# Two more feed-forward steps before the inverse-transform stage, and a different spread of start-up work, in an FFT-mixing and feed-forward kernel

## Chip, cores and metric

One Trainium2 chip, one of its cores. The metric is the device time of one execution in microseconds, the median of several runs. The engines are named as in the profile: PE is TensorE's matmuls, PEld its weight loads, DVE VectorE, ACT ScalarE, POOL GpSimd, SP SyncE (here it only issues transfers).

## What is computed

Eight batches of 3072 tokens with 256 channels. Each batch goes through a real FFT over its tokens, a complex 256x256 channel mix with bias and soft threshold, an inverse FFT, and then a feed-forward block of width 2048:

```python
X = np.fft.rfft(x, axis=1)
Yr = Xr @ w_r - Xi @ w_i + b_r
Yi = Xr @ w_i + Xi @ w_r + b_i
Y  = soft_threshold(Yr, 0.01) + 1j * soft_threshold(Yi, 0.01)
y  = np.fft.irfft(Y, n=3072, axis=1)
h  = y @ w_in                      # 256 -> 2048
out = (h * np.tanh(softplus(h))) @ w_out   # 2048 -> 256
```

`w_in` and `w_out` are in double precision, the rest in float32.

## The kernel before

The FFT of one batch is written as four stages of small matmuls, held as lists of items by `chain(b)`, with the result of each of the first three stages stored to a scratch in DRAM and read back in another order:

- Stage one (items A, 7 of two matmul groups): loads x, writes the scratch `s1`. PSUM tile `psa`.
- Stage two (12 items B, each followed one item later by an item M that mixes the channels): reads `s1`, multiplies (`psb`, then `psk` and `psp`, or `psm` in the first batch), adds bias, thresholds on DVE (L481 to L483), and stores `y` to the scratch `s3`: four transfers for most items (L572).
- Stage three (13 items C): each reads `s3` with four transfers (L612), is split on DVE into a high part (`hi`, L195) and a low part (`lo`, L198), multiplied (`psc`, three matmuls, L634), copied by ACT and stored to `s2`.
- Stage four (12 items F, called columns here): one transfer from `s2` (L652) and one of constants `vt`; a split on DVE; matmuls `psf` (L677, L678); then on DVE `eo`, `yt` and `yl` (L681 to L687), with ACT's `cor` and `yh` in between. This gives the activations `yh`, `yl` of the feed-forward block.

All products of float32 values are built from a high and a low part, so splits on DVE precede most matmuls.

The feed-forward block of the current batch runs at the same time as the FFT of the next one. The main loop counts steps `t`, 96 for a batch (six chunks of tokens by 16 slices of the width 2048). A step issues, in this order: `ffn1` (six matmuls into `hp`, L759, then an activation `s` on ACT); every second step `split_g` (the split of `s` into `gh` and `gl` on DVE, L773 and L774, a pair of steps at a time); then one piece of the FFT; then `ffn2` of four steps earlier (twelve matmuls into `acc`, L790). The FFT pieces come from two generators made by `run_chain`. `extra` brings one column of the current batch's FFT; two are created in each of five chunks (`tt % 16` is 2 or 8). Its loads are issued at creation, its split three steps later, its matmuls two steps after that. `gen` brings stages one to three, and the first two columns, of the next batch. In a step in which `extra` issues its matmuls, `gen` is not advanced.

`run_chain` walks the stages. At the start of a stage it issues the first loads (three items ahead), then yields some empty steps, in which only feed-forward work is issued; then it issues the first two splits, yields again, and then issues one item's matmuls per step, with the loads three and the splits two items ahead. The number of empty steps is this line; `k == 2` is stage three, and `gap` is 2 in the main loop:

```python
for _ in range(gap + (2 if k == 2 else 1 if last else 0) if gap else 0):
    yield None
```

So four empty steps stand before the first splits of stage three, and one between them and its first matmuls. This place occurs seven times, in the FFTs of batches 2 to 8, during the feed-forward work of batches 1 to 7. The FFT of the first batch runs alone ahead of the main loop, with `gap=0`. DVE works on the feed-forward weights in that time: `aux_steps(n)` issues n small DVE operations that turn double-precision weights (`raw`) into high and low parts in `win` and `wout`, 97 of them at most. `on_seg(k)` issues a fixed number at a stage's start, and `PACE[k]` is the number per piece of stage k. `aux_load`, `load_mix` and `load_bias` issue the transfers of raw weights (POOL), mixing weights (SP) and bias (POOL).

Of the kernel before, what the change touches and what calls it, by code (L numbers as in the profile page):

```python
# [127 lines left out]
def fft_mix_ffn_kernel(ctx: ExitStack, tc: tile.TileContext, x, w_r, w_i, b_r, b_i, w_in, w_out,  # L128
# [35 lines left out]
    def f32(ap):  # L164
        return ap.bitcast(F32)
# [27 lines left out]
    def split(src, hi, lo, eng="v"):  # L193
        if eng == "v":
            nc.vector.tensor_copy(out=hi, in_=src)  # L195
        else:
            nc.scalar.activation(out=hi, in_=src, func=ACTF.Copy)  # L197
        nc.vector.tensor_tensor(out=lo, in0=src, in1=f32(hi), op=ALU.subtract)  # L198
# [10 lines left out]
    def setup_dft():  # L209
        nc.gpsimd.dma_start(out=fa, in_=c_fa)  # L210

    def setup_u():
        nc.gpsimd.dma_start(out=uu, in_=c_u)
# [3 lines left out]
    def load_mix():  # L217
        for k in range(2):
            t = p_y.tile([128, 2, 512], F32, tag=("yh", "yl")[k], name="wraw").rearrange("p a f -> p (a f)")[:, 0:512]
            nc.sync.dma_start(out=t[:, 0:256], in_=w_r[k * 128:(k + 1) * 128, :])  # L220
            nc.sync.dma_start(out=t[:, 256:512], in_=w_i[k * 128:(k + 1) * 128, :])
            mixraw.append(t.rearrange("p (s c) -> p s c", s=2))

    def load_bias():
        nc.gpsimd.dma_start(out=bias[:, 0, :], in_=b_r.rearrange("(o c) -> o c", o=1).to_broadcast([128, DM]))
        nc.gpsimd.dma_start(out=bias[:, 1, :], in_=b_i.rearrange("(o c) -> o c", o=1).to_broadcast([128, DM]))

    def setup_mix():
        for k in range(2):
            src = mixraw[k]  # L230
            hi, lo = wmix[:, k, 0, 1:3, :], wmix[:, k, 1, 1:3, :]
            split(src, hi, lo, "s")
            for s in range(2):
                nc.scalar.activation(out=wmix[:, k, s, 0, :], in_=f32(wmix[:, k, s, 2, :]), func=ACTF.Copy, scale=-1.0)
# [63 lines left out]
    def weight_jobs():  # L298
        def w1(k, n):
            sl = slice(n * 512, (n + 1) * 512)  # L300
            return (w_in.bitcast(I32)[k * 128:(k + 1) * 128, n * 1024:(n + 1) * 1024],
                    *(win[:, k, s, sl].rearrange("p (a c) -> p a c", a=2) for s in range(2)), False)

        def w2(n):
            return (w_out.bitcast(I32)[n * 256:(n + 1) * 256, :].rearrange("(k p) c -> p k c", p=128),
                    *(wout[:, 2 * n:2 * n + 2, s, :] for s in range(2)), True)

        order = [w1(0, 0), w1(1, 0), w1(0, 1), w1(1, 1), w2(0), w2(1), w1(0, 2), w1(1, 2), w2(2), w2(3),
                 w1(0, 3), w1(1, 3), w2(4), w2(5), w2(6), w2(7)]
        return [FromDouble(n, *a) for n, a in enumerate(order)]  # L310
# [15 lines left out]
    def tick():  # L326
        while pend:
            pend.pop(0)()
# [378 lines left out]
    def run_chain(segs, ahead_n=3, ahead_a=2, cla=2, gap=0, hold=None, on_seg=None):  # L707


        for k, seg in enumerate(segs):  # L710
            while hold is not None and k == len(segs) - 1 and hold():
                yield None
            n = len(seg)
            at = [0, 0, 0]
            la, pla = (ahead_a, 1) if k == 0 and n == 7 else (ahead_n, 2)

            def ahead(i):
                for s, (d, f) in enumerate(((la, "load"), (cla, "cload"), (pla, "prep"))):
                    while at[s] < min(n, i + d):
                        getattr(seg[at[s]], f)()  # L720
                        at[s] += 1

            while at[1] < min(n, cla):
                seg[at[1]].cload()
                at[1] += 1
            while at[0] < min(n, la):
                seg[at[0]].load()
                at[0] += 1
            if on_seg is not None:
                on_seg(k)  # L730
            last = k == len(segs) - 1
            for _ in range(gap + (2 if k == 2 else 1 if last else 0) if gap else 0):
                yield None
            while at[2] < min(n, pla):
                seg[at[2]].prep()
                at[2] += 1
            for _ in range((2 if last or k == 1 else 1) if gap else 0):
                yield None
            for i in range(n):
                ahead(i + 1)  # L740
                for f in seg[i].mm:
                    tick()
                    f()
                    yield k
            tick()
# [59 lines left out]
    with tc.manual_schedule():  # L805
        setup_dft()
        aux = weight_jobs()
        n_raw = [0]

        def aux_load(m):  # L810
            while n_raw[0] < min(m, len(aux)):
                aux[n_raw[0]].load()
                n_raw[0] += 1

        def aux_run():
            for n, job in enumerate(aux):
                aux_load(n + 1)
                for k, _ in enumerate(job.work(aux[n - 1] if n else None)):
                    if k == 5:
                        aux_load(min(n + (4 if n + 3 <= N_EARLY else 3), 16 if started[0] else N_EARLY + 1))  # L820
                    yield
            yield from aux[-1].finish()

        aux_gen = aux_run()
        n_aux = [0]

        def aux_steps(m):
            for _ in range(m):
                if started[0] or n_aux[0] < 9 * N_EARLY - 2:
                    next(aux_gen, None)  # L830
                    n_aux[0] += 1

        def on_seg(k):
            if k == 1:
                setup_mix()
                aux_steps(4)
            elif k == 2:
                aux_steps(12)
            elif k == 3:
                aux_steps(10)  # L840

        PACE = (1.6, 0.9, 1.6, 2)
        first = chain(0)
        cnt = 0
        owed = 0.0
        for k in run_chain(first, ahead_n=6, ahead_a=3, cla=3, on_seg=on_seg):
            cnt += 1
            if cnt in (2, 5, 9):
                aux_load(1 + (cnt > 2) + 2 * (cnt > 5))
            if cnt == 7:  # L850
                load_mix()
                load_bias()
            if cnt == 11:
                for it in first[1][:3]:
                    it.cload()
            if cnt == 20:
                setup_u()
            if cnt == 57:
                for it in first[3]:
                    it.cload()  # L860
            if cnt > 4:
                owed += PACE[k]
            while owed >= 1:
                aux_steps(1)
                owed -= 1
        aux_steps(9 * len(aux))
        started[0] = True

        LAG = 4
        NT = NCH * KFF  # L870
        NS = 6 * KFF
        gen = None
        extra = None
        for t in range(NT + LAG):
            tt = t % NS
            b = t // NS
            if t < 18:
                aux_steps(3)
            if t == 18:
                aux_steps(18)  # L880
                mix_gauss()
            if NB > 1 and 12 <= t < 60 and t % 4 == 0:
                copy_consts((t - 12) // 4)
            if t < NT:
                if tt == 0:
                    gen = run_chain(chain(b + 1), gap=2, hold=lambda: hold[0]) if b + 1 < NB else None
                hold = [tt < 5 * KFF + 2]
                ffn1(t)
                c = tt // KFF
                if tt % KFF in (2, 8) and c < 5:  # L890
                    extra = run_chain([[item_f(b, 2 * c + 2 + (tt % KFF) // 8)]], gap=2)
            if t % 2 == 0 and t // 2 - 1 in s_t:
                split_g(t // 2 - 1, t < 18)
            did = None
            if extra is not None:
                did = next(extra, -1)
                if did == -1:
                    extra = did = None
            if did is None and gen is not None and t < NT:
                did = next(gen, -1)  # L900
                if did == -1:
                    gen = None
            if t < NT and tt == NS - 1 and gen is not None:
                hold = [False]
                for _ in gen:
                    pass
                gen = None
            if t >= LAG:
                ffn2(t - LAG)
# [26 lines left out]
```

## Time and profile before

| | |
|---|---|
| median of 3 runs | 2877.02 us (2873.92 to 2881.51) |
| the profiled execution: time / span | 2874.97 us / 2873.1 us |
| mean granted TensorE clock | 0.984 |
| busy: PE, PEld, DVE, ACT, POOL | 97%, 87%, 66%, 33%, 2% |
| chain that ended last: PE / DMA / DVE / SP's queue | 89% / 4% / 3% / 2% |
| HBM traffic over the span | 96 GB/s |

The busy row is a mean over two different parts. The first batch's FFT (up to about 159 us) has PE at 60 to 70 per cent; from then on PE is busy in nearly every slice. Idle time of DVE, ACT or POOL costs nothing there unless PE waits for it. So the lines to read are those that tell where PE stood still, how long, and at what clock it started again.

### The profile page before, as it was taken

To read this page: it belongs to the slowest core of one execution; us is meant where nothing else is said; L and a number is where in the kernel's file an instruction comes from. 1 tells how busy PE (TensorE), PEld (TensorE's weight loads), DVE (VectorE), ACT (ScalarE), POOL (GpSimd) and SP (SyncE) were. 2 spreads that over 40 slices of the span, in tenths; PEclk is the share of its full clock that TensorE was granted. 3 is DMA by queue.
4 is the path that set the end of the run, shared out by engine and by line. 5 is a ranking of instruction groups with operands and counts; after the bars stand their busy time and mean duration, and the time that the engine had idled before them with its cause. 6 is when DMAs were issued, how large, how long until landed. Compare 5 with 4: busy or idle time off the path is not lost.

```text
span 2873.1 us, 44977 instructions
## 1 busy us (share of the span) xinstructions
PE 2779.6 (97%) x17812; PEld 2497.7 (87%) x17812; DVE 1891.6 (66%) x3116; ACT 946.0 (33%) x1844; POOL 60.4 (2%) x112
## 2 busy tenths in 40 slices
PE   6779999999999999999999999999999999999999
PEld 4468989899898998889989899888988899899998
DVE  6887765677657775567755777567765677654443
ACT  3333333233233333333333333323333233332222
POOL 1400000000000000000000000000000000000000
PEclk9789999999999999999999999999999999999999
DMA  7754433333224223242233322433223232221010
GB/s 216 204 151 118 116 91 114 94 98 91 75 88 126 85 78 89 90 123 78 68 108 98 106 78 68 130 92 90 85 76 119 87 106 82 80 82 45 23 38 15
DMA packets 171176, 273.13 MB, mean 95 GB/s; under 512 B 22902, under 2 KB 67974, under 8 KB 170582
## 3 DMA queue, kind: packets, MB, share of 16 engines
q1 hardware_dynamic: 146902, 222.78, 26.0%
q10 hardware_dynamic: 13856, 25.17, 3.1%
q0 software_dynamic: 10208, 22.31, 2.8%
q8 instruction: 140, 2.29, 0.3%
q14 instruction: 70, 0.57, 0.1%
HBM read 169.49 MB, written 107.23 MB: 96 GB/s over the span
## 4 chain that ended last, share of the span: by engine, by line
PE 89%; DMA 4%; DVE 3%; SPq 2%; issue 1%; ACT 1%; POOL 0%; ACTq 0%; DVEq 0%
PE acc L790 37%; PE hp L759 35%; PE psp L526 4%; PE psc L634 2%; PE psa L361 2%; SPq L612 2%; PE psk L507 2%; PE psf L677 2%; PE psb L442 2%; DMA ld<-s 1%; DMA lds<-in_x_dram 1%; PE psf L678 1%; PE psb L444 1%; DVE lo L198 1%; PE psb L427 0%
## 5 line engine op out<-in xcount | busy, mean ns | idle before, releaser
L790 PE MATMUL acc<-wout,gh 128*128 128x256 f32 x6144 | 1145.7, 284 | 0.0
L759 PE MATMUL hp<-yh,win 128*128 128x512 f32 x3072 | 1089.5, 395 | 5.2 <-ACT yh L686 4.6
L790 PEld LDWEIGHTS acc<-wout,gh 128*128 128x128 f32 x6144 | 975.4, 189 | 42.0 <-issue 6.0
L764 ACT ACTIVATE s<-hp 128x512 f32<-128x512 f32 x768 | 459.6, 598 | 1451.4 <-PE hp L759 1341.8
L790 PE MATMUL acc<-wout,gl 128*128 128x256 f32 x3072 | 870.1, 283 | 0.0
L759 PEld LDWEIGHTS hp<-yh,win 128*128 128x128 f32 x3072 | 581.8, 189 | 105.1 <-ACT yh L686 4.8
L759 PE MATMUL hp<-yl,win 128*128 128x512 f32 x1536 | 606.5, 395 | 0.0
L790 PEld LDWEIGHTS acc<-wout,gl 128*128 128x128 f32 x3072 | 582.3, 190 | 0.0
L774 DVE TENSOR_TENSOR gl<-s,gh 128x1024 fp32r<-128x1024 f32 x384 | 470.6, 1225 | 82.2 <-PE acc L790 43.4
L773 DVE CAST gh<-s 128x1024 fp32r<-128x1024 f32 x376 | 259.3, 690 | 332.8 <-ACT s L764 332.7
L759 PEld LDWEIGHTS hp<-yl,win 128*128 128x128 f32 x1536 | 290.8, 189 | 36.3 <-DVE yl L687 0.4
L198 DVE TENSOR_TENSOR lo<-ld,hi 120x512 fp32r<-120x512 f32 (+3 forms) x390 | 269.8, 692 | 29.6 <-ACT hi L197 16.9
L195 DVE CAST hi<-ld 120x512 fp32r<-120x512 f32 (+2 forms) x367 | 154.3, 420 | 71.8 <-DMA ld<-s 71.8
L681 DVE TENSOR_TENSOR eo<-psf,cor 128x256 f32<-128x256 f32 x192 | 77.3, 423 | 152.1 <-ACT cor L680 151.4
L526 PE MATMUL psp<-wmix,xh 128*128 128x256 f32 x672 | 133.0, 281 | 0.0
L634 PE MATMUL psc<-hi,uu 120*120 120x512 f32 (+1 forms) x224 | 91.6, 423 | 39.6 <-DVE hi L195 24.1
L361 PE MATMUL psa<-hi,fa 120*120 120x512 f32 (+1 forms) x224 | 96.3, 436 | 19.2 <-DMA fa<-in_c_fa_dram 7.2
L526 PEld LDWEIGHTS psp<-wmix,xh 128*128 128x128 f32 x672 | 108.9, 188 | 3.7
L687 DVE TENSOR_TENSOR yl<-yt,yh 128x512 fp32r<-128x512 f32 x96 | 66.5, 693 | 67.0 <-ACT yh L686 67.0
L686 ACT ACTIVATE yh<-yt 128x512 fp32r<-128x512 f32 x96 | 60.7, 632 | 140.0 <-DVE yt L684 140.0
L481 DVE TENSOR_TENSOR y<-psp,y 128x512 f32<-128x512 f32 x84 | 58.1, 691 | 69.9 <-PE psp L526 68.5
L374 DVE TENSOR_TENSOR eva<-psa,s2nd 120x512 f32<-120x512 f32 (+1 forms) x112 | 72.9, 685 | 47.1 <-ACT s2nd L366 27.4
(108 smaller groups left out, 2445.2 us busy)
## 6 DMA issues: line engine op xcount, KB each, us to landing
ld<-s SPq DMA_DIRECT2D x185, 256.0 KB
out_dram<-ot SPq DMA_DIRECT2D x48, 512.0 KB
ld<-in_x_dram SPq DMA_DIRECT2D x90, 240.0 KB
vt<-v_scr SPq DMA_DIRECT2D x84, 256.0 KB
s<-ev ACTq DMA_DIRECT2D x89, 240.0 KB
s<-y SPq DMA_DIRECT2D x330, 64.0 KB
ld<-s SPq DMA_DIRECT2D x350, 60.0 KB
s<-eva SPq DMA_DIRECT2D x84, 240.0 KB
```

The lines of the kernel that those rows point to most:

```text
L195: nc.vector.tensor_copy(out=hi, in_=src)
L198: nc.vector.tensor_tensor(out=lo, in0=src, in1=f32(hi), op=ALU.subtract)
L361: nc.tensor.matmul(out=ps[:K], lhsT=fa[:K, h, s, col:col + K], rhs=m[:K], start=n == 0, stop=n == 2)
L374: nc.vector.tensor_tensor(out=evv[e][:K], in0=it.ps[:K].rearrange("p (j c) -> p j c", j=2), in1=s2nd[:K].rearrange("p (j c) -> p j c", j=2 ...
L526: nc.tensor.matmul(out=it.ps[:, ri * 256:(ri + 1) * 256], lhsT=m[:, c, 130 - ri * 128:258 - ri * 128], rhs=wmix[:, c, s, 2 * ri, :], start ...
L634: nc.tensor.matmul(out=ps[:K, sl], lhsT=uu[:K, var, s, :K], rhs=m[:K, sl], start=n == 0, stop=n == 2)
L681: nc.vector.tensor_tensor(out=eo[:, c], in0=ps[:, :, 0], in1=cor, op=ALU.add)
L759: nc.tensor.matmul(out=hp, lhsT=win[:, k, s, f * 128:(f + 1) * 128], rhs=m[:, k, :], start=n == 0, stop=n == 5)
L764: nc.scalar.activation(out=s_t[t // 2][:, t % 2, :], in_=hp, func=ACTF.Mish)
L773: nc.vector.tensor_copy(out=gh, in_=s)
L774: nc.vector.tensor_tensor(out=gl, in0=s, in1=f32(gh), op=ALU.subtract)
L790: nc.tensor.matmul(out=p, lhsT=m[:, t % 2, o:o + 128], rhs=wout[:, f, s, :], start=f == 0 and h == 0 and n == 0, stop=last and h == 1 and ...
```

## The change

In `run_chain` the number added to `gap` at stage three goes from 2 to 4: six empty steps in place of four. In the first batch, `on_seg` issues 6 and 14 weight operations at the start of stages two and three in place of 4 and 12, and stage three takes 1.3 per piece in place of 1.6. The third and fourth raw weight blocks are asked for at the start of stage two at the latest, in place of after the ninth piece; the mixing weights after the eighth piece in place of the seventh; the bias after the twelfth in place of the seventh; the first constants of stage two after the twelfth in place of the eleventh.

```diff
@@ run_chain
-            for _ in range(gap + (2 if k == 2 else 1 if last else 0) if gap else 0):
+            for _ in range(gap + (4 if k == 2 else 1 if last else 0) if gap else 0):
                 yield None
@@ on_seg
             if k == 1:
+                aux_load(4)
                 setup_mix()
-                aux_steps(4)
+                aux_steps(6)
             elif k == 2:
-                aux_steps(12)
+                aux_steps(14)
             elif k == 3:
                 aux_steps(10)
 
-        PACE = (1.6, 0.9, 1.6, 2)
+        PACE = (1.6, 0.9, 1.3, 2)
@@ the loop over the first batch's pieces
             cnt += 1
-            if cnt in (2, 5, 9):
-                aux_load(1 + (cnt > 2) + 2 * (cnt > 5))
-            if cnt == 7:
+            if cnt in (2, 5):
+                aux_load(1 + (cnt > 2))
+            if cnt == 8:
                 load_mix()
+            if cnt == 12:
                 load_bias()
-            if cnt == 11:
                 for it in first[1][:3]:
                     it.cload()
```

DVE, in the step where stage three's first splits stood, in the FFT of batch 3. `ld_7980` is the column of `extra`, `ld_7938`, `ld_7943` and `ld_7948` are the first three items of stage three, `ld_8090` the fourth. Before:

```order
L195 CAST hi_8053<-ld_7980 128x512
L198 TENSOR_TENSOR lo_8054<-ld_7980,hi_8053 128x512
L195 CAST hi_8057<-ld_7938 120x512
L198 TENSOR_TENSOR lo_8058<-ld_7938,hi_8057 120x512
L195 CAST hi_8061<-ld_7943 120x512
L198 TENSOR_TENSOR lo_8062<-ld_7943,hi_8061 120x512
L773 CAST gh_8086<-s_8025 128x1024
L774 TENSOR_TENSOR gl_8087<-s_8025,gh_8086 128x1024
L195 CAST hi_8095<-ld_7948 120x512
```

Here the first two items of stage three are split right behind the column's split. Now, at the same place:

```order
L195 CAST hi_8053<-ld_7980 128x512
L198 TENSOR_TENSOR lo_8054<-ld_7980,hi_8053 128x512
L773 CAST gh_8078<-s_8025 128x1024
L774 TENSOR_TENSOR gl_8079<-s_8025,gh_8078 128x1024
L681 TENSOR_TENSOR eo_8104<-psf_8105,cor_8110 128x256
L681 TENSOR_TENSOR eo_8104<-psf_8113,cor_8118 128x256
L683 TENSOR_TENSOR yt_8121<-eo_8104 128x2x128
L684 TENSOR_TENSOR yt_8121<-eo_8104 128x2x128
L687 TENSOR_TENSOR yl_8103<-yt_8121,yh_8102 128x2x256
L773 CAST gh_8147<-s_8076 128x1024
L774 TENSOR_TENSOR gl_8148<-s_8076,gh_8147 128x1024
L195 CAST hi_8155<-ld_7938 120x512
```

The column's split stays where it was; a `gh`/`gl` pair, the column's remaining work and another pair now stand between it and the first split of stage three.

PE at the same kind of place (here the first of the seven), as a piece of the difference: the end of a step's `hp`, and what followed it.

```order
 L759 MATMUL hp<-yl,win 128x512
 L759 MATMUL hp<-yh,win 128x512
-L634 MATMUL psc<-hi,uu 120x512
-L634 MATMUL psc<-lo,uu 120x512
-L634 MATMUL psc<-hi,uu 120x512
 L790 MATMUL acc_4229<-wout,gh 128x256 x2
 L790 MATMUL acc_4229<-wout,gl 128x256
```

The first `psc` leaves this step. Counted over the whole rows, it now comes three steps later: this one, the column's step, in which `gen` is not advanced, and one more are without it. All later pieces of that FFT come two steps later, and the matmuls of its second column are followed by two steps of the batch without FFT work in place of four.

POOL at the start of the first batch, before:

```order
L210 DMA fa<-in_c_fa_dram 120x672
L261 DMA raw<-in_moe_w_in_dram 128x1024 x2
L225 DMA bias<-in_b_r_dram 128x256
L226 DMA bias<-in_b_i_dram 128x256
L261 DMA raw<-in_moe_w_in_dram 128x1024 x2
L406 DMA tt<-in_c_t_dram 128x512 x3
L261 DMA raw<-in_moe_w_out_dram 128x2x512
L406 DMA tt<-in_c_t_dram 128x512 x2
L261 DMA raw<-in_moe_w_out_dram 128x2x512
L406 DMA tt<-in_c_t_dram 128x512
```

And now (`tt` are constants of stage two):

```order
L210 DMA fa<-in_c_fa_dram 120x672
L261 DMA raw<-in_moe_w_in_dram 128x1024 x4
L225 DMA bias<-in_b_r_dram 128x256
L226 DMA bias<-in_b_i_dram 128x256
L406 DMA tt<-in_c_t_dram 128x512 x3
L261 DMA raw<-in_moe_w_out_dram 128x2x512 x2
L406 DMA tt<-in_c_t_dram 128x512 x3
```

The bias goes behind two raw blocks, and a sixth raw block moves ahead of two `tt` transfers. SP's order in the first batch is the same in both kernels.

## Rows read from the trace of the kernel before

**Rows 1.** The page's first line.
```profile
span 2873.1 us, 44977 instructions
```
**Rows 2.** Waits of PE from 170 us on: us in total, times, longest.
```profile
PE psc L634 <- DVE hi L195: 24.1, 7, 4.2
```
**Rows 3.** Windows, two steps at the first, second and third place, and all seven's sum.
```profile
core 0: us, PE busy (x) PEld busy (x) DVE busy (x) ACT busy (x) POOL busy (x), PEclk, DMA share, GB/s
421.85:432.71 10.86, 7.76 (x50) 6.47 (x48) 7.22 (x14) 2.45 (x5) 0.00 (x0) 1.00 0.50 155
764.52:777.65 13.13, 9.14 (x50) 7.61 (x49) 7.24 (x14) 2.45 (x5) 0.00 (x0) 0.87 0.56 174
1109.45:1124.19 14.74, 10.52 (x49) 8.77 (x48) 7.25 (x14) 2.45 (x5) 0.00 (x0) 0.77 0.54 165
...
sum 90.60, PE 65.57 PEld 54.86 DVE 50.73 ACT 17.16 POOL 0.00; mean PE 9.37 PEld 7.84 DVE 7.25 ACT 2.45 POOL 0.00
```
**Rows 4.** Windows: two undisturbed steps of the same make; the first 20 us.
```profile
1138.28:1145.51 7.23, 7.23 (x49) 6.57 (x48) 3.45 (x7) 2.46 (x5) 0.00 (x0) 1.00 0.44 128
...
0.00:20.00 20.00, 7.41 (x12) 3.04 (x12) 3.97 (x6) 4.49 (x7) 6.96 (x16) 1.00 0.92 250
```
**Rows 5.** Timeline of SP's queue, second place: start, us, what.
```profile
753.66 9.96 SPq L612 DMA_DIRECT2D ld<-s  x12
```
**Rows 6.** Chain that ended last, first batch and second place: start us, us, what.
```profile
128.52 6.03 DMA ld<-s
...
764.19 4.30 DMA ld<-s
...
774.09 1.38 PE hp L759 x6
...
776.35 1.46 PE acc L790 x12
777.81 1.40 PE hp L759 x6
779.21 0.70 PE psc L634 x3
779.91 1.43 PE acc L790 x12
```
**Rows 7.** Timeline of PE: start, us, instruction, [idle before <-releaser].
```profile
426.28 0.50 PE L634 MATMUL psc<-hi,uu 120*120 120x512 f32 x1 [2.87 <-DVE hi L195]
...
427.56 0.40 PE L790 MATMUL acc<-wout,gh 128*128 128x256 f32 x2
...
770.06 0.78 PE L634 MATMUL psc<-hi,uu 120*120 120x512 f32 x1 [3.99 <-DVE hi L195]
...
842.86 0.29 PE L677 MATMUL psf<-vt,hi 128*128 128x256 f32 x1
```
**Rows 8.** Timeline of DVE.
```profile
49.30 0.69 DVE L198 TENSOR_TENSOR lo<-lds,hi 128x512 fp32r<-128x512 f32 x1 [1.18 <-ACT hi L197]
...
768.52 0.43 DVE L195 CAST hi<-ld 128x512 fp32r<-128x512 f32 x1 [8.23 <-DMA ld<-s]
...
769.59 0.42 DVE L195 CAST hi<-ld 120x512 fp32r<-120x512 f32 x1
...
771.72 0.69 DVE L773 CAST gh<-s 128x1024 fp32r<-128x1024 f32 x1
...
773.65 0.42 DVE L195 CAST hi<-ld 120x512 fp32r<-120x512 f32 x1
...
776.41 0.81 DVE L681 TENSOR_TENSOR eo<-psf,cor 128x256 f32<-128x256 f32 x2 [1.62 <-ACT cor L680]
...
781.72 0.69 DVE L198 TENSOR_TENSOR lo<-ld,hi 120x512 fp32r<-120x512 f32 x1
...
846.33 0.69 DVE L687 TENSOR_TENSOR yl<-yt,yh 128x512 fp32r<-128x512 f32 x1 [0.70 <-ACT yh L686]
```
**Rows 9.** Timeline of POOL, end of the first batch's stage three.
```profile
135.66 0.53 POOL L261 DMA_DIRECT2D raw<-in_moe_w_in_dram  x1 [5.52 <-DVE win L293]
```

## Prediction, made before the changed kernel was run

> **What bounds the kernel now.** I read the page first: PE is busy nearly all of the 2873.1 us span [rows 1], so the question is where it stood still. The list of PE's waits from 170 us on has one large entry: seven times, 24.1 us in all and 4.2 at most, PE waits for a split on DVE before the first matmul of stage three [rows 2]. Seven is the number of FFTs that run beside feed-forward work, so it is once in each, at the place that the first edit touches.
>
> Second, the cost of such a place. I cut out two steps: from the start of the step that holds the first `psc` to the start of the step behind the column's. The seven stretches sum to 90.60 us [rows 3]. The same two steps, later in a batch where nothing waits, take 7.23 us [rows 4]. The seven places therefore lose 90.60 - 7 x 7.23 = 40.0 us, not 24.1. The rest is clock: 1.00 at the first place, but means of 0.87 and 0.77 at the next two, so that matmuls behind the wait run partly at the lower of the two levels, 1.2 GHz [rows 3]. At the first place the wait was 2.87 us and no clock was lost [rows 7]; the places with lost clock waited longer.
>
> Third, who is late. DVE stood still 8.23 us for a load, then split a 128-row tile and only then the 120-row tile that PE wanted [rows 8]. The 128-row tile is not stage three's: it is the column of `extra`. SP had issued twelve loads of stage three in 9.96 us [rows 5] ahead of the column's load, which then took 4.30 us [rows 6]. So DVE, which works in order, is held by the column's load, with stage three's own tiles long there.
>
> **The first edit.** It moves the split and the matmuls of stage three later, but neither the column's load nor its split: the program's order ahead of that split is unchanged on SP and DVE. DVE is released at the same time as before. The question is how much DVE must do from there to the first split of stage three, and when PE now comes for it.
>
> PE: a step without FFT work takes 1.40 + 1.43 = 2.83 us; the column's step 1.38 + 0.88 + 1.46 = 3.72, where 0.88 is the `psf` matmuls between the end of `hp` (774.09 + 1.38) and `acc` at 776.35 [rows 6]. From the start of the step that used to wait to the first `psc` there are now a free step, the column's step, a free step and one `hp`: 2.83 + 3.72 + 2.83 + 1.40 = 10.8 us.
>
> DVE: the column's split begins w after that step's start, where w is the old wait of the place: at the second place 768.52 - 764.52 = 4.00 for a wait of 3.99 [rows 3, 7, 8]. Behind it come, in the new order, the column's split, 769.59 - 768.52 = 1.07; a `gh`/`gl` pair, 773.65 - 771.72 = 1.93; then `eo`, `yt`, `yl`, a second pair and the high part of a stage-three split, which stand in the trace of before in just this order, from 776.41 to the low part's start at 781.72: 5.31, ACT's part in it included [rows 8]. Together 8.3 us.
>
> So the new wait is w + 8.3 - 10.8 = w - 2.5 at each place; the largest becomes 1.8 us. Summed: 24.1 - 7 x 2.47 = 6.8 us. Whatever PE loses earlier, at the column's own matmuls, lies inside that figure, since it is counted from DVE's end. When the high part comes just in time, the low part is late for the second matmul: at the first place `psc` took 427.56 - 426.28 = 1.28 us against 0.70 undisturbed [rows 6, 7], so 0.58 more, seven times 4.1. I charge no clock, because the new waits are all shorter than the 2.87 us of the first place, which cost none. Remaining loss 6.8 + 4.1 = 10.9; **gain 40.0 - 10.9 = 29.1 us.** The bounds are a gain of 40.0 (nothing left) and of 24.1 + 4.1 less, 11.8 (each place keeps w and the late low part, but no lost clock). I take 29.1 because every term has its own row.
>
> A rule of the Trainium skill gives another time for one link. The page "DMA: Bandwidth & Descriptors", section "Anatomy of one DMA — SWDGE (gpsimd) path", fits a transfer's time as about 2.0 us plus its bytes over 436 GB/s, which makes 2.6 us for the column's 256 KB, and would leave next to no new wait, a gain of 40. It was fitted for transfers issued from GpSimd. The row of this SP transfer says 4.30 [rows 6], and the sum goes by that.
>
> The two added steps come off the end of the batch. The second column's matmuls there start at 842.86, and its last result is ready at 846.33 + 0.69, 4.2 us later [rows 7, 8]. From those matmuls to the next batch's first `hp` there will be 0.88 + 1.46 + 2 x 2.83 = 8.0 us. So 3.8 us are left, and it costs nothing. Loads of stage four and of the next x are issued relative to those steps and move with them.
>
> **The edits in the first batch.** The raw weights are not really later: the weight work itself asks for the third and fourth block at its sixth operation, ahead of the ninth piece, in both versions. What changes on POOL is that the bias goes behind those two blocks, and a sixth block (512 KB) ahead of two `tt` (256 KB each), where it must wait for the first block to be finished. That takes one `tt` out of the first 20 us, in which the DMA engines are 0.92 busy at 250 GB/s [rows 4]: 256 KB there are 1.0 us. It may cost as much as 768 KB at that rate, 3.0, when both come out again near the start of stage two. The two operations more at that stage's start fall into an idle of 1.18 us on DVE, which waits there for ACT's split of the load [rows 8]; their cover is the scratch's round trip, and without it they would cost about 1.2. The two more at the start of stage three run while its loads are on the way; uncovered they cost at most 1.4. Within stage three four operations fewer, each at most the 0.69 of a two-input operation of that size [rows 8], can give 2.8; against it, a raw block that waited 5.52 us on POOL for DVE [rows 9] now stands ahead of the last item's two half loads and the columns' `vt`, which bounds the loss at 5.5. I take 0, between -3.8 and +11.1, since most of what moved is not waited for.
>
> **The sum.** The profiled execution took 2874.97 us, 1.9 above its span; less 29.1 it is 2845.9. It lies 2.05 below the median of the runs, 2877.02, so for a median I say 2877.02 - 29.1 = **2848 us**. About 0.3% (8.6 us) is what a measurement of this kernel can tell from no change.
>
> **Rivals.**
> - Nothing is left of the wait: 2877 - 40 = 2837. For it: the 0.5 MB output store is issued right behind the column's load, and if that load lands 2.5 us sooner, DVE keeps ahead of PE. Against: nothing on SP ahead of it changes. Chance 0.10. The Trainium skill's fit above is this case.
> - DVE's backlog is longer than 8.3, for instance because ACT's parts come late behind its activations: with 10.8 each place keeps w, the gain is 11.8, 2865. Against: the 5.31 were measured with ACT just as loaded. Chance 0.10.
> - Both that and a first batch that loses its 11.1 us leave a gain of 0.7, 2876: no change. Chance 0.05. If only the late loading does nothing, as the order says, the forecast stands.
> - Slower: the wait moves to the fourth item of stage three. Its loads need the buffer of an earlier tile, now freed late. They are issued from w + 8.9 on (the two parts of the first item's split), take 4 x 0.83 = 3.3 [rows 5], and the item's `psc` comes three steps of 1.40 + 0.70 + 1.43 behind the first one [rows 6]. With w = 3.4 that is 10.8 + 1.0 + 0.6 + 10.6 = 23.0, less 0.5 for the split, against 15.6 for the last issue: a landing of up to 6.9 us is hidden. The column's load took 4.30, the longest in the chain of stage three of the first batch 6.03 [rows 6]. To be slower by over 0.3% it would need 6.9 + (29.1 + 8.6) / 7 = 12.3 us. Chance 0.04.
>
> **How the numbers follow.** The forecast, a gain of 22 to 36, has 0.71. Faster by over 0.3%: forecast, nothing left and the longer backlog, 0.91. Same 0.05, slower 0.04. The range 2836 to 2860 holds nearly all of the forecast's cases with the first batch's bounds, most of the first rival and a little of the second, about 0.8.
>
> **What would show it.** Right: seven waits before the first `psc` remain, together about 7 us, each 0.4 to 1.8, for the DVE split; DVE still waits 7 to 8 us for the column's load at the same place; windows of the same content (the old two steps plus two free ones) at clock 1.00; no PE wait at the batch's end. The first `hp` still starts near 159 us. Wrong: waits of 3 us or lost clock there, a new wait at the fourth item or at a batch's first `hp`, or a first batch that moves by more than 4 us.

## The result, and the profile after

The changed kernel takes **2850.28 us** (median of 4 runs, 2847.72 to 2853.11) against 2877.81 for the kernel before (4 runs): a ratio of 0.9905 with a 95% interval of 0.9888 to 0.9922, a gain of 27.5 us. The forecast was 2848, from a gain of 29.1. The profiled execution took 2847.72 us; its span and mean clock (0.988, was 0.984) come with this line of the page, which answers to [rows 1] (the span is the time from the first to the last instruction):

```profile
span 2845.9 us, 45013 instructions
```

PE's waits from 170 us on, the answer to [rows 2] (us in total, times, longest). The first two rows are all that is left before stage three; the next two belong to the matmuls of stage four:

```profile
PE psc L634 <- DVE hi L195: 2.2, 7, 0.3
PE psc L634 <- DVE lo L198: 1.6, 7, 0.2
...
PE psf L678 <- DVE lo L198: 0.7, 2, 0.3
...
PE psf L677 <- DVE hi L195: 0.4, 1, 0.4
```

A wait in this list is only the part in which PE was idle. What a place costs is read from windows, as in [rows 3]. Here each window is the same two steps plus the two added free ones, from the start of the step that used to wait; undisturbed they would take 7.23 + 2 x 2.83 = 12.89 us. Columns: window, its length, PE busy, granted clock, DMA share, GB/s.

```profile
424.91:438.83 13.92, 13.40 (x86) 1.00 0.27 85
764.99:779.70 14.71, 13.80 (x86) 1.00 0.34 115
1105.86:1121.08 15.22, 13.95 (x85) 1.00 0.37 115
...
sum 99.74, PE 94.90; mean PE 13.56
```

The clock is 1.00 in all seven, and 99.74 - 7 x 12.89 = 9.5 us are lost, where 40.0 were before. So the places gave back 30.5.

The timeline of DVE at the second place, beside [rows 8] (start, us, instruction, [idle before <-releaser]):

```profile
768.73 0.43 DVE L195 CAST hi<-ld 128x512 fp32r<-128x512 f32 x1 [7.97 <-DMA ld<-s]
...
769.80 0.69 DVE L773 CAST gh<-s 128x1024 fp32r<-128x1024 f32 x1
...
771.74 0.75 DVE L681 TENSOR_TENSOR eo<-psf,cor 128x256 f32<-128x256 f32 x2
...
776.52 0.42 DVE L195 CAST hi<-ld 120x512 fp32r<-120x512 f32 x1
776.98 0.69 DVE L198 TENSOR_TENSOR lo<-ld,hi 120x512 fp32r<-120x512 f32 x1
```

DVE is still held 7.97 us by the column's load, and from there to the low part of stage three's first split it needs 776.98 - 768.73 = 8.25 us. The prediction had 8.3.

The first batch lost what the places did not keep. The first matmul of stage two, first before and then after:

```profile
49.31 0.80 PE L427 MATMUL psb<-tt,hi 128*128 128x256 f32 x2 [9.59 <-ACT hi L197]
```

```profile
51.55 0.80 PE L427 MATMUL psb<-tt,hi 128*128 128x256 f32 x2 [12.15 <-ACT hi L197]
```

And the first `hp`, which ends the first batch, before and after:

```profile
158.94 0.80 PE L759 MATMUL hp<-yh,win 128*128 128x512 f32 x1 [4.60 <-ACT yh L686]
```

```profile
163.17 0.79 PE L759 MATMUL hp<-yh,win 128*128 128x512 f32 x1 [4.59 <-ACT yh L686]
```

So the trace splits the gain in two: 4.2 us lost ahead of the first `hp`, and behind it (2873.1 - 158.94) - (2845.9 - 163.17) = 31.4 gained, of which 30.5 lie in the seven places. This split, "ahead of the first `hp`" and "behind it", is used for every run below, because the first part scatters by itself: in seven traces with the unedited first batch (before and six of the experiments) the first `hp` starts between 158.94 and 162.89. The 4.2 alone are therefore no price of the edits; the part on the first batch takes them apart.

### The profile page after: what moved, and what is told of

Read it like the earlier page. It is cut to its first block, busy times and chain, and to the rows that moved or that the text cites. A ratio compares the mean times of both kernels' runs of the same rounds, so it can differ in the third digit from the quotient of the medians.

```text
span 2845.9 us, 45013 instructions
## 1 busy us (share of the span) xinstructions
PE 2768.7 (97%) x17812; PEld 2490.2 (88%) x17812; DVE 1890.9 (66%) x3116; ACT 942.3 (33%) x1844; POOL 60.9 (2%) x112
## 4 chain that ended last, share of the span: by engine, by line
PE 90%; DVE 4%; DMA 3%; issue 1%; SPq 1%; ACT 1%; POOL 0%; ACTq 0%; DVEq 0%
PE acc L790 37%; PE hp L759 35%; PE psp L526 4%; PE psc L634 2%; PE psa L361 2%; PE psk L507 2%; PE psf L677 2%; PE psb L442 2%; DMA ld<-s 1%; DMA lds<-in_x_dram 1%; SPq L612 1%; PE psf L678 1%; DVE lo L198 1%; PE psb L444 1%; PE psm L543 1%
## 5 line engine op out<-in xcount | busy, mean ns | idle before, releaser
L198 DVE TENSOR_TENSOR lo<-ld,hi 120x512 fp32r<-120x512 f32 (+3 forms) x390 | 269.7, 692 | 29.1 <-ACT hi L197 16.4
L677 PE MATMUL psf<-vt,hi 128*128 128x256 f32 x384 | 95.9, 326 | 9.2 <-ACT hi L197 7.2
```

The costliest lines, as they stand in the source:

```text
L677: nc.tensor.matmul(out=ps[:, p], lhsT=it.hi[:, q:q + 128], rhs=it.v[:, p], start=True, stop=False)
```

## Experiments

Two questions: what of the gain belongs to which edit, and what holds DVE at the place. The theory is the prediction's: SP issues the column's load last, DVE works in order, so stage three's splits wait behind the column's. The rivals: the load is late whatever its queue; or the wait moves on with every step added.

| run | empty steps added (2 before), edits in the first batch | median, us | ratio, 95% interval | gain behind first `hp` |
|---|---|---|---|---|
| after | 4, all edits | 2850.28 | 0.9905 [0.9888, 0.9922] | 31.4 |
| gap4_only | 4, none | 2847.72 | 0.9904 [0.9891, 0.9918] | 30.0 |
| first_only | 2, all edits | 2881.07 | 1.0020 [1.0011, 1.0029] | -1.6 |
| raw6_back | 4, without the sixth block's move | 2847.27 | 0.9904 [0.9890, 0.9917] | 28.9 |
| gap3_only | 3, none | 2838.28 | 0.9876 [0.9861, 0.9891] | 37.7 |
| col_pool | 2, none; column's load on POOL | 2842.49 | 0.9881 [0.9866, 0.9896] | 35.8 |
| gap6_only | 6, none | 2852.26 | 0.9915 [0.9900, 0.9930] | 25.4 |
| gap3_pool | 3, none; column's load on POOL | 2838.17 | 0.9864 [0.9847, 0.9880] | 39.7 |
| gap3_first | 3, without the sixth block's move | 2840.36 | 0.9876 [0.9862, 0.9891] | 37.5 |
| gap3_all | 3, all edits | 2843.12 | 0.9891 [0.9877, 0.9906] | 35.8 |
| gap3_none_again | 3, none | 2839.91 | 0.9879 [0.9863, 0.9896] | 36.9 |
| gap3_first_again | 3, without the sixth block's move | 2843.78 | 0.9891 [0.9876, 0.9906] | 38.0 |
| gap3_loads | 3, later loads only | 2841.31 | 0.9876 [0.9859, 0.9892] | 37.0 |

The last column is the kernel before's 2714.16 us from its first `hp` to the end of its span, less the same of the profiled run. The kernel before took 2877.81 beside the changed kernel, 2875.24 beside gap4_only, first_only, raw6_back and gap3_only, 2876.71 beside col_pool, gap6_only, gap3_pool and gap3_first, 2874.64 beside gap3_all, gap3_none_again and gap3_first_again, and 2877.03 beside gap3_loads.

### One part of the change alone

gap4_only is the kernel before with the first edit alone, first_only the change without it:

```diff
-            for _ in range(gap + (2 if k == 2 else 1 if last else 0) if gap else 0):
+            for _ in range(gap + (4 if k == 2 else 1 if last else 0) if gap else 0):
```

> Only the two empty steps ahead of stage three, the first batch as before. If the seven places alone carry the gain (40.0 us lost before, 9.4 lost after, read from the two traces), it is 30.6 us faster than before, about 2847, and about 3 faster than the whole change; its first hp starts at 159 us. If the first batch's edits carry a part of the gain, it is slower than the whole change, above 2850.

> Only the first batch's edits, four empty steps as before. My theory: the first hp starts 4.2 us late, at about 163 us, of which some 3 remain at the first place; the seven places wait 24.1 us as before; total 2 to 4 us slower than before, about 2881. Rival: the late first batch was chance of one execution, then within 1 us of before.

The first edit alone gives 27.5 us, the others alone cost 5.8 (3.2 to 8.3 by the interval; 10 runs against 14). So the whole gain is the two empty steps. By their ratios, 0.9904 and 0.9905, gap4_only and the whole change can't be told apart, and each interval is some 8 to 10 us wide. That is no evidence against a cost of the rest: gap4_only's first `hp` started at 161.65, 2.7 us later than in the kernel before's trace, with the same instructions ahead of it on every engine. Behind that, its gain is 30.0.

### Three empty steps in place of four

```diff
-... gap + (2 if k == 2
+... gap + (3 if k == 2
```

> Five empty steps in place of four, the first batch as before. DVE's order is then column split, one gh/gl pair, stage three's first splits: they end w + 3.5 after the step's start, PE comes at 2.83 + 3.72 + 1.40 = 8.0, so with w up to 4.2 there is no wait for them; only the column's own matmuls wait, 0.8 and 1.0 us at the second and third place. Gain about 38 us, 2839. Rival, that the number of steps is what matters (more steps cover more): a gain between 0 and 30.6, half of it about 15, 2863.

One step fewer is 9.4 us faster than gap4_only on the same chip, and it beats both kernels. DVE at the second place shows why:

```profile
765.39 0.43 DVE L195 CAST hi<-ld 128x512 fp32r<-128x512 f32 x1 [8.47 <-DMA ld<-s]
...
766.46 0.69 DVE L773 CAST gh<-s 128x1024 fp32r<-128x1024 f32 x1
...
768.39 0.42 DVE L195 CAST hi<-ld 120x512 fp32r<-120x512 f32 x1
768.85 0.69 DVE L198 TENSOR_TENSOR lo<-ld,hi 120x512 fp32r<-120x512 f32 x1
...
770.52 0.75 DVE L681 TENSOR_TENSOR eo<-psf,cor 128x256 f32<-128x256 f32 x2
```

Stage three's split now stands behind one `gh`/`gl` pair, but ahead of the column's `eo`, `yt`, `yl` and the second pair. From the column's split to the low part it is 768.85 - 765.39 = 3.46 us instead of 8.25. PE comes for it 2.83 + 3.72 + 1.40 = 8.0 us after the start of the step that used to wait, instead of 10.8. So the fourth step gives PE 2.83 us more time and DVE 4.8 us more work in front of the split. PE's `psc` has no idle before it:

```profile
770.32 0.40 PE L634 MATMUL psc<-hi,uu 120*120 120x512 f32 x1
```

### More empty steps

gap6_only has `6 if k == 2` at the same line.

> The kernel before with six added empty steps in place of two, nothing else. Theory (each empty step shortens the wait by a step's 2.83 us until the end of the batch has no time left): no wait before the first psc, but the second column of the next batch now ends too late for that batch's first hp. From the trace, its results come 4.2 us after its matmuls, and 2.3 us of work are left for them, so about 1.9 us of wait at each of seven batch starts, 13 us in all, against the 37.7 us that the places give: main loop 24 to 25 us less than before, about 2851 us. Rival (only the wait at the places counts, the end has room): about 2838 us, and no wait of hp on yl or yh after the first batch.

The rival that more is better, or harmless, falls: 2852.26. The wait before `psc` is gone, and PE now waits where the batch begins, for the last column (waits of PE from 170 us on; the first row is seven batch starts, the second the `yl` behind them):

```profile
PE hp L759 <- ACT yh L686: 6.9, 7, 1.0
...
PE hp L759 <- DVE yl L687: 1.6, 7, 0.2
```

With four added steps neither row is there. So the end of a batch has room for four, as the prediction had it (3.8 us left), and not for six.

### What holds DVE: the column's load behind twelve others

col_pool leaves the four empty steps of before and changes the queue of one load, for the FFTs of batches 2 to 8:

```diff
-            nc.sync.dma_start(out=it.t, in_=s2[...])
+            (nc.gpsimd if b > 0 and nb >= 2 else nc.sync).dma_start(out=it.t, in_=s2[...])
```

> The kernel before (four empty steps) with one edit: the load of a column of extra is issued from POOL instead of SP, so that it no longer stands behind stage three's twelve loads on SP; nothing of the order on PE or DVE is changed. Theory (DVE is held by the column's load, because that load is issued last): DVE's stop of 7 to 8 us in front of the column's split goes, the seven waits before the first psc (24.1 us in the kernel before) go with it, and the main loop gets as short as with three added empty steps, 37.7 us less than before: about 2838 us. Rival (the load is late because the sixteen DMA engines are busy with stage three's loads, whichever queue it comes from): the stop stays above 5 us, the waits stay above 15 us, and the time stays above 2860 us.

The first place is a control: its column belongs to the first batch's FFT, which the edit leaves on SP. The windows are those of [rows 3], the old two steps (length, PE busy, clock, DMA share, GB/s):

```profile
423.95:436.27 12.32, 9.29 (x50) 0.86 0.50 149
768.08:775.30 7.22, 7.22 (x50) 1.00 0.78 247
1107.11:1114.33 7.22, 7.22 (x49) 1.00 0.71 212
...
sum 55.67, PE 52.64; mean PE 7.52
```

At the first place DVE is held as before and PE waits 2.80 us. It loses 12.32 - 7.23 = 5.1 us, more than the 10.86 - 7.23 = 3.6 of the kernel before [rows 3], because here the clock fell, to a mean of 0.86, behind a wait of nearly the same length. At the six others not 0.01 us is lost, with the order on PE and DVE untouched. PE's waits have one large row for it, one wait instead of seven:

```profile
PE psc L634 <- DVE hi L195: 2.8, 1, 2.8
```

The rival (the transfer is late because the DMA engines are busy) falls, since they are busier in these windows than in those before. What changed is when the load is issued. On POOL, which has nothing else to do, the second place's load goes out as soon as its buffer is free; on SP, in the changed kernel, it stands behind the twelve. Timeline of POOL in col_pool, then of SP's queue in the same run, then the chain that ended last in the changed kernel:

```profile
733.45 0.57 POOL L652 DMA_DIRECT2D ld<-s  x1 [37.39 <-DVE lo L198]
```

```profile
732.12 24.21 SPq L572 DMA_DIRECT2D s<-y  x12
757.20 10.02 SPq L612 DMA_DIRECT2D ld<-s  x12
```

```profile
765.34 3.37 DMA ld<-s
```

The first is 34.6 us ahead of the step that starts at 768.08, the last 0.4 us behind the start of its step, 764.99. Of those 34.6 the twelve loads of stage three take 10.0. The rest is what stands ahead of them in SP's queue, stage two's stores of `y` in 24.21 us, with the waits for the `y` in between. A load that passed the twelve alone would come 10 us sooner, more than the 8 us that DVE is held; no run shows that. The miss of 4.5 us against the expected 2838 is the first place, which the edit does not reach: 5.1 us.

gap3_pool has both, three empty steps and the load on POOL.

> Three added empty steps and the column's load from POOL, both at once. Theory (with three, DVE has stage three's splits done before PE comes, and nothing is left at the places): the same as three empty steps alone, 2838 us within 3 us. Rival (with three, something of the column's lateness is still paid, at the psf matmuls or later): 4 us or more below 2838 us.

The time is that of three empty steps, 2838.17. Behind the first `hp` its gain is 39.7, 2.0 more than gap3_only's and about the 40.0 us that the prediction counted as lost at the places: next to nothing is left there to gain.

### What the first batch costs

raw6_back is the change, but the sixth raw block stays behind two `tt`, as before (`cnt` counts the pieces; the block is asked for at the 17th):

```diff
-            while n_raw[0] < min(m, len(aux)):
+            while n_raw[0] < min(m, len(aux), 5 if cnt < 17 else 16):
...
+            if cnt == 17:
+                aux_load(6)
```

> The whole change, but the sixth raw weight block issued behind two constants of stage two again, as before, with everything else as in the change. If that block's transfer is what delays the last store of stage one (5.0 us in place of about 2), stage two's first matmul comes at 49 us again in place of 51.6, and the total is 2 to 4 us below the whole change, about 2847. If the moved DVE operations or the later bias cause the loss, the first hp stays at 163 us and the total at 2850.

Stage two starts at 49.41 again, as without the edits, so the block's move is what put its start off by 2.2 us. Against gap4_only on the same chip, 2847.27 to 2847.72, the edits that are left show no cost. gap3_first is the same on three empty steps.

> Three added empty steps with the first-batch edits of the change, but the sixth raw block again behind two tt. Theory (apart from that block the edits of the first batch are worth nothing): 2838 us within 2 us. Rival (the lower clock behind the 1.6 us wait for tt in stage two, seen in all three traces with these edits and not in that of three empty steps alone, belongs to the edits): first hp 1.5 to 2.5 us later than with three empty steps alone, 2840 us. Second rival (the edits do help once the block is out of the way): below 2836 us.

Inconclusive by its time, 2840.36, since its interval is all but that of gap3_only. Its first `hp` (161.15) lies inside the scatter. So three kernels were timed on one chip, the third of them with the diff of gap3_first:

> The changed kernel with three added empty steps in place of four, so with all of its first-batch edits, the sixth raw block ahead of two tt among them. Run on one chip with the two kernels below. Theory (the sixth block ahead of the tt holds stage two's start up by 2 us, and the rest of the first-batch edits is worth nothing): 2.0 us slower than the same kernel without first-batch edits, its first psb near 51.5 us. Rival (as the first-batch edits alone gave, 2881.07 against 2875.24 us): 4 to 6 us slower. Second rival (the later start is given back by the end of the first batch): within 1 us.

> Three added empty steps and no first-batch edit, again, as the other end of the comparison on this chip: about 2838 us. Its first psb is expected near 49.5 us; its first hp, which lay between 158.9 and 162.9 us in six traces with the same first batch, anywhere in there.

> Three added empty steps and the first-batch edits without the sixth block's move, again, on this chip: the same as without any first-batch edit within 1 us if the block is all that they cost; 2 us slower if stage two's lower clock is theirs too.

All the edits cost 3.2 us here (2843.12 against 2839.91), and the ones without the sixth block 3.9, where raw6_back beside gap4_only showed nothing. So the times leave open what the edits without the block cost, and the traces have to tell. They show one difference in stage two. Windows of the stretch from 79 us in the kernel before, then in the changed one (length, PE busy, clock, DMA share, GB/s):

```profile
79.00:82.00 3.00, 2.17 (x16) 1.00 0.86 238
82.00:85.00 3.00, 3.00 (x20) 1.00 0.58 135
```

```profile
79.00:82.00 3.00, 3.00 (x13) 0.58 0.65 186
82.00:85.00 3.00, 3.00 (x19) 0.85 0.63 175
```

In all six traces with the two added weight operations the clock from 79 to 82 us is 0.50 to 0.66; in all seven without a first-batch edit it is 1.00, and it stays so up to 88 us, also in those where the wait for a `tt` (below) ends only at 82 to 83 us. In the changed kernel the loss is 3 x 0.42 + 3 x 0.15 = 1.7 us; by the same windows to 88 us it is 3.4 in gap3_all. It follows a wait of PE for a `tt` (timeline of PE, before and after):

```profile
79.83 0.41 PE L430 MATMUL psb<-tt,hi 128*128 128x128 f32 x2 [1.35 <-DMA tt<-in_c_t_dram]
```

```profile
78.16 0.41 PE L430 MATMUL psb<-tt,hi 128*128 128x128 f32 x2 [1.61 <-DMA tt<-in_c_t_dram]
```

POOL issues a raw block directly ahead of a `tt`: at 74.29 us in the kernel before, behind the third item's stores, and at 72.66 in the changed one, behind the second item's, although its stage two began 2.2 us later. gap3_loads keeps the numbers of weight operations of before and takes the later loads alone:

```diff
-                aux_steps(6)
+                aux_steps(4)
...
-                aux_steps(14)
+                aux_steps(12)
...
-        PACE = (1.6, 0.9, 1.3, 2)
+        PACE = (1.6, 0.9, 1.6, 2)
```

> Three added empty steps and, of the first-batch edits, only the later loads (mixing weights, bias, stage two's first constants, and the third and fourth raw block); the numbers of weight operations (4, 12, 1.6 per piece) are those of before, so that the raw blocks stand between the tt of stage two as they did before. Theory (the two added weight operations bring a raw block one item earlier into stage two, its transfer makes a tt late, and PE's clock falls behind that wait): the clock between 79 and 85 us stays at 1.00 as in the seven traces without these edits, and the time is that of three empty steps alone, 2838 to 2840 us. Rival (the later loads themselves bring it): lower clock there, as in all six traces with all the edits, and 2841 to 2844 us.

The clock is back, and the raw block is behind the third item again (73.70 us):

```profile
79.00:82.00 3.00, 2.75 (x18) 1.00 0.76 198
82.00:85.00 3.00, 3.00 (x20) 1.00 0.71 165
```

So the lower clock belongs to the weight operations' numbers, not to the later loads, and the first `psb` is at 48.68, so the block's early place does too. The time, 2841.31, is between the two expectations and settles nothing; its ratio, 0.9876, is that of three steps alone. Why the clock falls behind the wait for the `tt` in these six traces and not in the others isn't shown.

What the whole cost is made of can be read by cutting the first batch at three marks: the first `psb`, the first store of `y` on POOL, and the last matmul of stage two, which starts at 103.55 in the kernel before and at 107.70 in the changed one. The first store, before and after:

```profile
64.97 1.05 POOL L572 DMA_DIRECT2D s<-y  x2 [9.99 <-DVE y L483]
```

```profile
67.02 1.03 POOL L572 DMA_DIRECT2D s<-y  x2 [10.53 <-DVE y L483]
```

| us | before | after | eight traces without the added weight operations | six traces with them |
|---|---|---|---|---|
| start of the first `psb` | 49.31 | 51.55 | 48.7 to 49.9 | 51.5 to 52.4; 49.4 to 49.6 without the block's move |
| from there to the first store of `y` | 15.66 | 15.47 | 15.5 to 15.7 in three, 17.8 to 18.2 in five | 15.4 to 15.8 in five, 17.6 in gap3_first_again |
| from there to the last matmul of stage two | 38.58 | 40.68 | 38.6 to 39.1 in seven, 39.6 in one | 40.6 to 40.9 in four, 42.4 and 42.5 in two |
| from there to the first `hp` | 55.39 | 55.47 | 54.2 to 56.5 | 55.2 to 55.6 in five, 57.8 in gap3_first_again |

So the 4.2 us of the changed kernel are 2.2 from the block and 2.1 from the rest of stage two, 1.7 of it by the clock windows above; the later loads and the edits of stage three show no cost. The run raw6_back has the 2.1 as well (40.63 in the third row), so moving the block back does not remove it. The second row is the scatter: it has two forms, whatever the edits, and gap3_first and gap3_first_again, the same kernel, have one each. In the longer form the `psm` matmuls start 0.43 us apart in place of 0.23. Timeline of PE in the kernel before and in gap3_none_again, an unedited first batch of either form:

```profile
54.54 0.62 PE L543 MATMUL psm<-wmix,xh 128*128 128x512 f32 x2
55.00 0.39 PE L543 MATMUL psm<-wmix,xl 128*128 128x512 f32 x1
```

```profile
55.16 1.05 PE L543 MATMUL psm<-wmix,xh 128*128 128x512 f32 x2
56.01 0.63 PE L543 MATMUL psm<-wmix,xl 128*128 128x512 f32 x1
```

In the traced executions this is also why raw6_back and gap4_only came out alike (first `hp` at 161.08 and 161.65): gap4_only has the longer form, 17.9, with 38.7 behind it, raw6_back the shorter, 15.8, with 40.6. What decides the form stays open, and so do the 2.5 us that gap3_first_again lost behind stage two.

## Why the prediction was right

**The places.** The step "new wait = w - 2.5" held, and with 0.58 for the late low part it holds place by place at the three checked here, with the w of the new run (the column's split less the start of the old waiting step): at the second place 768.73 - 764.99 = 3.74, so 3.74 - 2.47 + 0.58 = 1.85 against 14.71 - 12.89 = 1.82 measured. At the first, with the split at 427.85, it gives 1.05 against 1.03, and at the third, with it at 1110.10, 2.35 against 2.33. The remaining loss was 9.5 where 10.9 was forecast, because the w themselves came out smaller: they sum to 22.9 instead of 24.1. But the waits did not stand where the text looked for them. It said "together about 7 us" before the first `psc`; 3.8 stand there in two rows. The rest is paid at the column's own `psf` and in matmuls that are stretched by the late operand, as the sentence on the column's matmuls allowed.

**The clock.** "I charge no clock" held: 1.00 in all seven windows. Its reason, that the waits are shorter than the 2.87 us of the first place, "which cost none", was weaker than it looked. At that same place a wait of 2.80 us in col_pool and one of 2.85 in first_only did cost clock. Windows of some 6.3 us from the first `psc`, in the kernel before, col_pool and first_only (length, PE busy, clock, DMA share, GB/s):

```profile
426.28:432.60 6.32, 6.09 (x41) 1.00 0.43 131
```

```profile
428.31:434.60 6.29, 6.06 (x28) 0.73 0.45 134
```

```profile
430.70:437.00 6.30, 6.29 (x31) 0.74 0.44 128
```

So the one row that the step rested on was a lucky one. The new waits in the list were far from it, 0.4 us at most, and cost no clock.

**The end of the batch.** Charged at nothing, and there is no wait. gap6_only shows that this cover is thin.

**The first batch.** Here a step failed: "I take 0, between -3.8 and +11.1, since most of what moved is not waited for". It costs some 3 to 6 us (5.8 in first_only, 3.2 in gap3_all by the times), and the traces put 2.2 of it on the sixth block and 2.1 on stage two behind its first store. The term of 3.0 "when both come out again near the start of stage two" was the sign of it: stage two did start 2.2 us later. By the prediction's own signs, a first batch that moves by more than 4 us was one of being wrong, and it moved by 4.2. What the sum lacked is that the two added operations, priced by their own duration and their cover, also move the raw transfers that are tied to them, one item earlier into a stretch in which PE waits for `tt`. That the total came within 2.3 us is in part luck, by two misses of opposite sign: the places gave 1.4 more, and the first batch took away some 3 us that were charged at nothing.

**The rivals.** "Nothing is left" would have needed the column's load to land earlier. By the chain of the changed kernel it took 3.37 us, 0.9 less than before [rows 6], and DVE was held as long as before, since its issue is late. The page "DMA: Bandwidth & Descriptors" of the Trainium skill, section "Anatomy of one DMA — SWDGE (gpsimd) path", fits 2.0 us plus the bytes over 436 GB/s, an estimate of 2.6 us for it; col_pool, which issues it from POOL, shows a median of 3.4 over 70 such loads, so the trace does not agree. The longer backlog falls with the 8.25 us on DVE. The fourth item is late on DVE, and no row of PE's waits has it.

## What to carry to other kernels

When an engine that works in order is held by one load, look first at what its queue issued ahead of it: here another queue for one transfer gave 35.8 us behind the first batch, nearly the 37.7 of the best shift of the work that waited. When work is moved by whole steps, count on both sides what each step puts in front of it: the fourth empty step gave PE 2.83 us and DVE 4.8 us, and three were better than four. An operation that is hidden itself can still carry a transfer that is not, so its price is also the place to which that transfer goes.

## What was not expected of the hardware

The same first batch, instruction for instruction, ended between 158.94 and 162.89 us in seven traces, while the clean batches behind it repeat closely (gains of 37.7 and 36.9 for one kernel); a single trace does not price an edit of that part. Most of the scatter is the slower start of stage two: its `psm` matmuls run 0.43 us apart in some traces and 0.23 in others, and the granted clock from 55 to 58 us is 1.00 in both, so the clock of the profile doesn't show this loss. And the length of a wait alone did not tell whether the clock would fall behind it. A wait of 1.61 us for a `tt` was followed by a clock of 0.58, one of 1.67 at the same `tt` in gap3_none_again by 1.00; before `psc`, at the first place, 2.87 us were followed by 1.00 [rows 3, 7] and 2.80, in col_pool, by a mean of 0.73.
